# Two regroupings in one kernel: early weights copied behind key tiles, late weights split in place behind attention

## The chip, the cores and the metric

The kernel runs on one core of one Trainium2 chip. The metric is the time of the whole program on the device in microseconds, the median of several runs. TensorE (PE in the rows, its weight load PEld) multiplies, VectorE (DVE), ScalarE (ACT) and GpSimd (POOL) work on elements, and SyncE (SP) issues most of the DMAs.

## The reference: three layers behind each other

```python
# 1. linear attention, 8 batches x 8 heads x 576 tokens x 64
proj = x @ w_phi;  proj -= max(abs(proj))            # x = q, k;  128 features
phi  = concat(exp(proj), exp(-proj))
kv = k_phi^T v;  z = sum(k_phi);  out = (q_phi kv) / (q_phi z + 1e-6)
# 2. four attention experts on d = 512, top 2 of 4 by a gate
logits = x @ w_gate;  w = softmax over the top 2
y_e = softmax(causal(q_e k_e^T / 8)) v_e @ wo_e;     out = sum of w_e * y_e
# 3. token shift, then a gated two-layer map
xk = mu_k*x + (1-mu_k)*x_prev;  xr = mu_r*x + (1-mu_r)*x_prev
r = sigmoid(xr @ w_r);  v = relu(xk @ w_k)**2 @ w_v;  out = r * v
```

All is float32. The kernel keeps accuracy by splitting a float32 operand into a rounded high part (a copy to the type fp32r, mostly on ACT) and a low part (a subtraction on DVE or POOL) and adding three products (`mm3`).

## The kernel before

The program is written as streams of small stages, and `weave` draws from whichever stream is furthest behind. The streams are: `favors` (layer 1, batch by batch, first the keys as `k_unit`, then the queries as `q_unit`), `moe1` (layer 2 up to the values, in tasks `s_task` and `av_task`), `compose` and `decodes` (they build combined weights of layers 2 and 3 and write them to DRAM as `wf` and `wc`), `load_moe1` (the weights of q, k, v of layer 2), `gates_keys` (matmuls `rk`, results in a tile `z`, stored to `kd`), and `moe2` (the last products, `vacc`). A scheduler of the tile framework then puts each engine's instructions into one fixed order. On the chip each engine works through its own order and waits in place for what is not ready; so does the DMA queue on SP.

Three places matter here.

- **The first keys.** A unit covers two tiles of 128 tokens (the third of each five covers one). It loads `raw`, splits it into `hi` (ACT, L97) and `lo` (POOL, L100), projects into `pj` (PE, L288 to L290), takes the absolute maximum `m` and subtracts it to get `pm` (DVE, L298 and L300), takes two exponentials `ph` (ACT, L323 and L324), and multiplies by the values into `kv` (PE, L343). `raw` and `hi` have two buffers each, and the projection has two banks of PSUM, so that unit 3 waits for the subtraction of unit 1. In the same stretch `load_moe1` brings six pieces of weights (`wst1`) and copies each (ACT, 0.6 us) and subtracts (DVE), and `compose` splits `wo` and starts to decode.
- **The late weights.** When layer 1 is done its buffers are closed, the state is called `favored`, and a pool `pW` opens in the same place. Four matrices `wc` (j = 0, 1, 3, 4) are read in eight pieces through two staging buffers (tag `wst2`), copied to `wch` on ACT and subtracted into `wcl` on POOL, by `combo`, all in one go. From then on the third slice of `rk` (`sl == 2`) puts its `z` into the same two staging buffers, while the first and second slices use a ring of four (tag `e`):

```python
if sl == 2 and len(WC) >= 4:
    z = late['pW'].tile([P, 768], F32, name='z', tag='wst2', bufs=2)[:, :HC]
else:
    z = pR.tile([P, HC], F32, name='z', tag='e', bufs=4)
```

- **Attention.** A piece of attention weights `a` is scaled on POOL (L559), transposed on PE (L566), multiplied by the values (`av_task`, L601), and its result is evacuated by ACT into `yc` (in `evac`, L104) and added by DVE (L610).

Of the kernel before, what the change touches and what calls it, by code (L numbers as in the profile page):

```python
# [13 lines left out]
P = 128  # L14
# [62 lines left out]
def fused_kernel(ctx: ExitStack, tc: tile.TileContext, qT, kT, vx, wphi, wq, wk, wvg, wo, mu, w64, ident, cmask, tri, out):  # L77
# [24 lines left out]
    def evac(e, o, i):  # L102
        if e == 'a':
            nc.scalar.activation(o, i, AF.Copy)  # L104
        else:
            nc.vector.tensor_copy(o, i)
    state = {}

    def tg(n):
# [37 lines left out]
    def clear_pads():  # L147
        for t in K2Z:
            nc.gpsimd.memset(t[64:P, 0].bitcast(F32), 0.0)
            nc.gpsimd.memset(t[0:64, 1].bitcast(F32), 0.0)  # L150
        for t in VSP:
            nc.gpsimd.memset(t[64:P, 4].bitcast(F32), 0.0)
        for t in AT1:
            nc.gpsimd.memset(t[64:P, 1280:1600].bitcast(F32), 0.0)
        for t in YF:
            nc.gpsimd.memset(t[:, 0:1], 0.0)

    def load_moe1():
        for src, h, l, n in ((wq, wqh, wql, 'p a b c -> p (a b c)'), (wk, wkh, wkl, 'p a b c -> p (a b c)'), (wvg, wvh, wvl, 'p a b -> p (a b)')):
            hf, lf, sf = (h.rearrange(n), l.rearrange(n), src.rearrange(n))  # L160
            w = hf.shape[1] // 2
            for i in range(2):
                s_ = pA.tile([P, S], F32, name='wst1', tag='a', bufs=3)
                nc.sync.dma_start(s_[:, :w], sf[:, i * w:(i + 1) * w])
                split(hf[:, i * w:(i + 1) * w], lf[:, i * w:(i + 1) * w], s_[:, :w], 'a')
                yield 40

    def decode(pool, i, rawkw, sq, cost=1, pool_raw=None):
# [7 lines left out]
        if sq == 'a':  # L176
            nc.scalar.activation(hz, top, AF.Square)
        else:
            nc.gpsimd.tensor_mul(hz, top, top)
# [28 lines left out]
    def compose():  # L208
        sw = [pR.tile([P, 4, 256], F32R, name='sw', tag=f'y{h}') for h in range(2)]
        for i in range(2):  # L210
            st_ = pR.tile([P, 2, 256], F32, name='wof', tag='e', bufs=4)
            nc.sync.dma_start(st_, wo[:, 2 * i:2 * i + 2])
            split(sw[0][:, 2 * i:2 * i + 2], sw[1][:, 2 * i:2 * i + 2], st_)
            yield 1
# [48 lines left out]
    def favor(b):  # L263
        kvbank = {}

        def proj_stages(src, g, u, dst, first=False):
# [4 lines left out]
            def load():  # L271
                t_ = pF.tile([P, 256], F32, name='raw', tag='raw', bufs=2)
                nc.sync.dma_start(t_[:, :n], src[b, g, :, tl[0] * P:tl[0] * P + n])
                dst['raw'] = t_
# [19 lines left out]
            def norm():  # L294
                g = 2 * nt
                ps = dst['ps'][:, :g * P].rearrange('p (g f) -> p g f', f=P)
                m = pF.tile([P, 4], F32, name='m', tag='m', bufs=3)
                nc.vector.tensor_reduce(m[:, :g], ps, axis=AX.X, op=OP.max, apply_absolute_value=True)  # L298
                pm = pF.tile([P, 512], F32, name='pm', tag='pm', bufs=3)
                nc.vector.tensor_sub(pm[:, :g * P].rearrange('p (g f) -> p g f', f=P), ps, m[:, :g].unsqueeze(2).to_broadcast([P, g, P]))  # L300
                dst['pm'] = pm
# [3 lines left out]
        def k_unit(g, u):  # L305
# [13 lines left out]
            def norm2():  # L319
# [3 lines left out]
                nc.scalar.activation(kp[:, 0, :n], d['pm'][:, :n], AF.Exp)  # L323
                nc.scalar.activation(kp[:, 1, :n], d['pm'][:, :n], AF.Exp, scale=-1.0)  # L324
                d['kp'] = kp

            def kvmm(sel):
# [90 lines left out]
    def moe1():  # L418
# [167 lines left out]
        def av_task(b, e, hf):  # L586
# [19 lines left out]
            def ev():  # L606
                ps = d['ps']
                yc = pA.tile([64, 320], F32, name='yc', tag='a', bufs=3)
                evac('a', yc[:, :W], ps[64:P, :W])
                nc.vector.tensor_add(YF[ep][hr, 1 + q0:1 + q0 + W], ps[0:64, :W], yc[:, :W])  # L610

            def taps():
# [48 lines left out]
    def favors():  # L661
# [14 lines left out]
        state['favored'] = True  # L676
        pW = late['pW'] = ctx.enter_context(tc.tile_pool(name='pW', bufs=1))
        for j in (0, 1, 3, 4):
            for k in range(2):
                combo(j, k, 1, pW, pW, 768, 'wst2', 2)()  # L680
                yield 2000
    WC = {}

    def combo(j, k, n, pool, stage, w, tag, bufs):
# [31 lines left out]
    def gates_keys():  # L716

        def one(c):
# [3 lines left out]
            def unit(n):  # L722
# [9 lines left out]
                def ev():  # L732
                    if sl == 2 and len(WC) >= 4:
                        z = late['pW'].tile([P, 768], F32, name='z', tag='wst2', bufs=2)[:, :HC]
                    else:
# [60 lines left out]
    def moe2():  # L796
# [12 lines left out]
        def first():  # L809
            while not (done.get(0, 0) == NB and B - 1 in read and len(WC) == 4):  # L810
                yield None
# [163 lines left out]
    fs, ms, rk, m2 = (favors(), skewed(moe1()), skewed(gates_keys()), moe2())  # L975
    for _ in range(3):
        next(fs)
    for dst, src in ((idn, ident), (cm, cmask), (trs, tri), (mus, mu)):
        nc.sync.dma_start(dst, src)
    weave(tc, (fs, 0.0, 99.0 * 1000.0, lambda: -1000 if 'favored' in state else 0), (ms, 0.8, 72.0 * 1000.0, lambda: 0), (compose(), 0.35, 206.0 / 2.15, lambda: -1000), (decodes(24, NW), 2.55, 5.0 * 16 / 1.6, lambda: -1000), (load_moe1(), 0.45, 1000.0, lambda: 0), (rk, 2.6, 60.0 * 1000.0, lambda: -1000), (m2, 4.7, 1e6, lambda: 0), until=ms)  # L980
    phA.close()
    state['late'] = True
# [52 lines left out]
```

## Time and profile before

| what | us |
|---|---|
| median of three runs | 1247.85 (1245.38 to 1250.11) |
| the profiled execution | 1247.39 |
| its span on the core | 1245.4 |
| PE busy in the span | 1209.5 (97%) |
| DVE, ACT, POOL busy | 943.0, 817.4, 428.3 |
| chain that ended last | PE 81%, DVE 8%, DMA 4%, ACT 3%, POOL 2% |

The profiled execution lies 0.46 us under the median, and 2.0 us of it lie around the span. PE is busy nearly all the time, so what can be won is found where it sits idle, or where it works at the lower of its two clocks. The page's second part shows both in forty slices.

### The profile page before, as it was taken

The numbers are of one execution on the slowest core, as the hardware profiler recorded it, in microseconds if no ns is written. First come the engines' busy times: TensorE is split into PE (matmuls) and PEld (weight loads), VectorE is DVE, ScalarE is ACT, GpSimd is POOL, SyncE is SP. The second block draws the span as 40 slices with busy tenths as digits, with TensorE's granted clock in tenths as the row PEclk, the third lists the DMA queues.
The fourth block names the chain that finished last, engine by engine and source line by source line (L and its number), as shares of the span: only waits on it lengthen the run. The fifth ranks groups of instructions, "written<-read, shape, count | busy, mean of one in ns | idle before, by whom it ended". The sixth has DMA issues, their size and how long they took to land.

```text
span 1245.4 us, 26673 instructions
## 1 busy us (share of the span) xinstructions
PE 1209.5 (97%) x9014; PEld 1169.1 (94%) x9014; DVE 943.0 (76%) x2493; ACT 817.4 (66%) x2008; POOL 428.3 (34%) x630
## 2 busy tenths in 40 slices
PE   8999999999999999999999999989999999999998
PEld 7899889999999999999999999988898899999998
DVE  7875988878977777886888767857657687756766
ACT  6665767657767776775668767577758585456534
POOL 5541666445643333543444534342211100000000
PEclk9999999989999999999999999999999999999999
DMA  6332134312324444455355443575788998899843
GB/s 206 91 88 86 63 99 154 110 59 83 108 80 147 145 146 122 115 162 157 108 169 177 128 134 119 177 237 156 219 283 279 317 349 301 285 308 304 283 150 127
DMA packets 186919, 212.71 MB, mean 171 GB/s; under 512 B 34464, under 2 KB 170528, under 8 KB 186784
## 3 DMA queue, kind: packets, MB, share of 16 engines
q1 hardware_dynamic: 172960, 192.12, 49.1%
q10 hardware_dynamic: 13824, 18.88, 4.2%
q8 instruction: 73, 1.20, 0.4%
q14 instruction: 62, 0.51, 0.1%
HBM read 145.94 MB, written 65.01 MB: 169 GB/s over the span
## 4 chain that ended last, share of the span: by engine, by line
PE 81%; DVE 8%; DMA 4%; ACT 3%; POOL 2%; issue 2%; SPq 0%; POOLq 0%; ACTq 0%; DVEq 0%
PE rk L117 16%; PE vacc L909 13%; PE kv L343 10%; PE num L386 8%; PE qk L117 6%; PE vp L117 4%; PE yp L601 3%; PE at L566 3%; PE pj L288 3%; PE pj L290 2%; PE pj L289 2%; PE fo L117 2%; PE tq L370 2%; PE sc L528 2%; PE sc L529 2%
## 5 line engine op out<-in xcount | busy, mean ns | idle before, releaser
L559 POOL TENSOR_SCALAR a<-a,sv,gw 128x128 f32<-128x128 f32 (+4 forms) x160 | 107.3, 672 | 228.3 <-DVE sv L553 87.6
L100 POOL TENSOR_TENSOR lo<-raw,hi 128x256 fp32r<-128x256 f32 (+1 forms) x160 | 109.6, 688 | 181.2 <-ACT hi L97 167.9
L386 PE MATMUL num<-kvs,ph 128*128 128x65 f32 (+1 forms) x1280 | 142.0, 262 | 0.6 <-DVE xs L393 0.6
L386 PEld LDWEIGHTS num<-kvs,ph 128*128 128x128 f32 (+1 forms) x1280 | 137.1, 181 | 4.3 <-issue 1.2
L298 DVE TENSOR_REDUCE m<-pj 128x4 f32<-128x512 f32 (+1 forms) x160 | 100.7, 630 | 34.2 <-PE pj L290 32.8
L909 PE MATMUL vacc<-XT,wch 128*128 128x384 f32 x480 | 123.3, 334 | 0.7 <-DVE XT L100 0.7
L741 DVE TENSOR_TENSOR z<-rk,z 128x384 f32<-128x384 f32 x144 | 79.0, 551 | 39.6 <-PE rk L117 27.8
L548 ACT ACTIVATE a<-sc,sv 128x128 f32<-128x128 f32 (+2 forms) x192 | 98.2, 513 | 16.3 <-DVE sv L543 9.2
L300 DVE TENSOR_TENSOR pm<-pj,m 128x512 f32<-128x512 f32 (+1 forms) x160 | 100.1, 629 | 4.5 <-ACT ph L324 1.9
L288 PE MATMUL pj<-wph,hi 128*128 128x256 f32 x288 | 90.0, 313 | 2.7 <-DVE pm L300 1.6
L543 DVE TENSOR_REDUCE sv<-sc 128x1 f32<-128x128 f32 (+2 forms) x192 | 88.4, 468 | 5.0 <-PE sc L529 2.0
L97 ACT ACTIVATE XT<-kx 128x1536 fp32r<-128x1536 f32 x40 | 59.4, 1487 | 47.7 <-PE vacc L909 40.4
L100 DVE TENSOR_TENSOR XT<-kx,XT 128x1536 fp32r<-128x1536 f32 x40 | 70.2, 1754 | 25.7 <-ACT XT L97 25.6
L909 PEld LDWEIGHTS vacc<-XT,wch 128*128 128x128 f32 x480 | 86.8, 188 | 1.1 <-DVE XT L100 1.1
L290 PE MATMUL pj<-wph,lo 128*128 128x256 f32 x288 | 82.3, 286 | 0.3 <-POOL lo L100 0.3
L97 ACT ACTIVATE hi<-raw 128x256 fp32r<-128x256 f32 (+1 forms) x160 | 62.0, 392 | 31.4 <-PE pj L289 9.3
L289 PE MATMUL pj<-wpl,hi 128*128 128x256 f32 x288 | 81.8, 284 | 0.0
L909 PE MATMUL vacc<-XT,wcl 128*128 128x384 f32 x240 | 79.6, 334 | 0.0
L566 PE MATMUL at<-idn,a 128*128 128x128 f32 (+2 forms) x480 | 72.6, 260 | 6.1 <-POOL a L559 5.2
L743 ACT ACTIVATE z<-z 128x384 f32<-128x384 f32 x96 | 50.0, 521 | 34.0 <-DVE z L741 30.5
L582 ACT ACTIVATE at1h<-at 128x384 fp32r<-128x384 f32 (+3 forms) x128 | 53.4, 418 | 25.1 <-PE at L566 17.5
L583 DVE TENSOR_TENSOR at1l<-at,at1h 128x384 fp32r<-128x384 f32 (+3 forms) x128 | 59.1, 462 | 13.9 <-ACT at1h L582 12.4
(531 smaller groups left out, 3696.1 us busy)
## 6 DMA issues: line engine op xcount, KB each, us to landing
wt<-wf SPq DMA_DIRECT2D x216, 256.0 KB, 3.7
kd<-z ACTq DMA_DIRECT2D x96, 192.0 KB, 3.4
kx<-kd SPq DMA_DIRECT2D x21, 768.0 KB, 8.0
yd<-yt SPq DMA_DIRECT2D x16, 864.0 KB, 4.7
kd<-z SPq DMA_DIRECT2D x48, 192.0 KB, 4.4
zs<-kd SPq DMA_DIRECT2D x12, 768.0 KB, 7.5
out_dram<-o SPq DMA_DIRECT2D x24, 384.0 KB, 3.4
raw<-in_kT_dram SPq DMA_DIRECT2D x64, 128.0 KB, 2.3
```

What stands on the lines that cost most here:

```text
L97: nc.scalar.activation(hi, src, AF.Copy)
L100: (el or nc.vector).tensor_sub(lo, src, hi.bitcast(F32))
L117: nc.tensor.matmul(ps, a, m, start=first and i == 0, stop=last and i == n - 1)
L288: nc.tensor.matmul(o, hi[:, c], wph, start=True, stop=False)
L289: nc.tensor.matmul(o, hi[:, c], wpl, start=False, stop=False)
L290: nc.tensor.matmul(o, lo[:, c], wph, start=False, stop=True)
L298: nc.vector.tensor_reduce(m[:, :g], ps, axis=AX.X, op=OP.max, apply_absolute_value=True)
L343: nc.tensor.matmul(bank[:, r, :], d['kp'][:, r % 2, c0:c0 + P], v, start=new and r == 0, stop=end, skip_group_check=True)
L386: nc.tensor.matmul(ps[lo_:hi_, i, j, :], d['qp'][:, hf, c0 + lo_:c0 + hi_], kvs[hp, b][:, r * 65:(r + 1) * 65], start=hf == 0, stop=hf == 1)
L559: eng(asc).tensor_scalar(a[:m, :nk], a[:m, :nk], rc[:m], WT[b][:m, i, e:e + 1], op0=OP.mult, op1=OP.mult)
L566: nc.tensor.transpose(ps[:kw, jj * m:jj * m + m], d['a'][:m, jj * P:jj * P + kw], idn[:m, :m])
L909: nc.tensor.matmul(ps, a[:, f, dp], m[:, f], start=j in (0, 1, 5) and n == 0, stop=n == 11, skip_group_check=True)
```

## The change

Late weights: each of the four `wc` is now loaded whole into its low tile `l` by one DMA of 512 KB, without staging. The eight halves are put on a list. Each `av_task` takes one from the list right after its evacuation `yc`: a copy of `l` into `h` on ACT, ordered behind that evacuation, and a subtraction on POOL that overwrites `l` in place. What is left over at the end of attention is done there. The second and third slices of `rk` get a ring of four `z` of their own in `pW`, and the first slice alone keeps the ring `e`.

Early weights: the first batch's key units leave marks (their subtraction on DVE and second exponential on ACT). The six copies of `load_moe1`, the two splits of `wo` and the first squares of `decode` are ordered behind one mark each, from unit 4 on. The third unit's `raw` is loaded into the tile of `xs`, which is not yet in use, and its load is issued ahead of the constants. Two clears of `vsp` go from POOL to DVE.

```diff
+    marks = []
+    @contextmanager
+    def behind(n):
+        with ExitStack() as es:
+            for ins in marks[n]:
+                es.enter_context(tc.issue_after(getattr(ins, 'ins', ins)))
+            yield
...
         for t in VSP:
-            nc.gpsimd.memset(t[64:P, 4].bitcast(F32), 0.0)
+            nc.vector.memset(t[64:P, 4].bitcast(F32), 0.0)
...
     def load_moe1():
+        k = 4
...
-                split(hf[:, i * w:(i + 1) * w], lf[:, i * w:(i + 1) * w], s_[:, :w], 'a')
+                with behind(k):
+                    split(hf[:, i * w:(i + 1) * w], lf[:, i * w:(i + 1) * w], s_[:, :w], 'a')
+                k += 1
...
-            nc.scalar.activation(hz, top, AF.Square)
+            with behind(6 + i if i < 2 else 9):
+                nc.scalar.activation(hz, top, AF.Square)
...
-            split(sw[0][:, 2 * i:2 * i + 2], sw[1][:, 2 * i:2 * i + 2], st_)
+            with behind(5 + i):
+                split(sw[0][:, 2 * i:2 * i + 2], sw[1][:, 2 * i:2 * i + 2], st_)
...
-                t_ = pF.tile([P, 256], F32, name='raw', tag='raw', bufs=2)
+                extra = first and b == 0 and g == 0 and u == 2
+                t_ = pF.tile([P, 256], F32, name='raw', tag='xs' if extra else 'raw', bufs=1 if extra else 2)
...
+                if b == 0:
+                    marks.append((d['sub'], e_))
...
-                evac('a', yc[:, :W], ps[64:P, :W])
+                last = evac('a', yc[:, :W], ps[64:P, :W])
                 nc.vector.tensor_add(YF[ep][hr, 1 + q0:1 + q0 + W], ps[0:64, :W], yc[:, :W])
+                resplit(getattr(last, 'ins', last))
...
         for j in (0, 1, 3, 4):
+            h, l = (pW.tile([P, 1024], F32R, name=f'wc{x}{j}') for x in 'hl')
+            nc.sync.dma_start(l.bitcast(F32), wc[:, j].rearrange('p q n -> p (q n)'))
+            WC[j] = [x.rearrange('p (f d n) -> p f d n', f=4, d=2) for x in (h, l)]
             for k in range(2):
-                combo(j, k, 1, pW, pW, 768, 'wst2', 2)()
-                yield 2000
+                q = slice(512 * k, 512 * k + 512)
+                late['splits'].append((h[:, q], l[:, q]))
+            yield 2000
+    def resplit(ins=None):
+        if late.get('splits'):
+            h, l = late['splits'].pop(0)
+            with tc.issue_after(ins) if ins is not None else ExitStack():
+                nc.scalar.activation(h, l.bitcast(F32), AF.Copy)
+            nc.gpsimd.tensor_sub(l, l.bitcast(F32), h.bitcast(F32))
...
-                    if sl == 2 and len(WC) >= 4:
-                        z = late['pW'].tile([P, 768], F32, name='z', tag='wst2', bufs=2)[:, :HC]
+                    if sl and 'pW' in late:
+                        z = late['pW'].tile([P, HC], F32, name='z', tag='z', bufs=4)
...
-    for _ in range(3):
+    for _ in range(4):
         next(fs)
...
+    while late['splits']:
+        resplit()
```

The change adds lines, so line numbers of the changed kernel differ: L323 and L324 become L336 and L337, the late copies of L97 become L709, and L743 and L744 become L771 and L772.

ACT, from its first key unit, before (`wqh` and `wkh` are copies of early weights, `hi` and `ph` belong to key units):

```order
L97 ACTIVATE hi<-raw 128x256 x2
L97 ACTIVATE hi<-raw 128x128
L97 ACTIVATE hi<-raw 128x256
L323 ACTIVATE ph<-pm 128x512
L324 ACTIVATE ph<-pm 128x512
L97 ACTIVATE wqh<-wst_879 128x512
L97 ACTIVATE wqh<-wst_975 128x512
L323 ACTIVATE ph<-pm 128x512
L324 ACTIVATE ph<-pm 128x512
L97 ACTIVATE wkh<-wst_1074 128x512
L97 ACTIVATE hi<-raw 128x256
```

The same place now:

```order
L97 ACTIVATE hi<-raw 128x256 x2
L97 ACTIVATE hi<-raw 128x128
L97 ACTIVATE hi<-raw 128x256
L336 ACTIVATE ph<-pm 128x512
L337 ACTIVATE ph<-pm 128x512
L97 ACTIVATE hi<-raw 128x256
L336 ACTIVATE ph<-pm 128x512
L337 ACTIVATE ph<-pm 128x512
L336 ACTIVATE ph<-pm 128x256
L337 ACTIVATE ph<-pm 128x256
L97 ACTIVATE hi<-raw 128x256 x2
L336 ACTIVATE ph<-pm 128x512
```

The copies of `wqh` and `wkh` stood from the first unit's exponentials on; now none of them stands before the fifth unit's.

ACT, where layer 1 has ended, before (`wch` is a copy of a late weight, `a` an exponential of attention, `qs` an evacuation of q):

```order
L97 ACTIVATE wch_13198<-wst_13200 128x512
L97 ACTIVATE wch_13198<-wst_13267 128x512
L548 ACTIVATE a,sv<-sc,sv 64x512
L548 ACTIVATE a,sv<-sc,sv 64x64
L582 ACTIVATE at1h<-at 128x4x128
L451 ACTIVATE qs<-qk 64x288 x4
L582 ACTIVATE at1h<-at 128x4x64
L451 ACTIVATE qs<-qk 64x288 x2
L97 ACTIVATE wch_13330<-wst_13332 128x512
```

The first copy as it stands now, in a later stretch of attention (`yc` is an evacuation of attention, `kd` a store of `z`):

```order
L104 ACTIVATE yc<-yp 64x256
L709 ACTIVATE wch_13198<-wcl_13199 128x512
L773 DMA kd_89<-z 128x384
L597 ACTIVATE at1h<-at 128x4x128
L771 ACTIVATE z<-z 128x384
L563 ACTIVATE a,sv<-sc,sv 128x128
L772 ACTIVATE z<-z 128x384
```

Before, two copies stood behind each other and further ones a few places on; now one stands behind an evacuation, and the next is some twenty rows away.

SP, the loads of late weights, before (`wt` are weights of `rk`, `yc_` its inputs, `wst` the staging buffers):

```order
L689 DMA wst_13411<-wc 128x512
L713 DMA yc__12109<-yd_69 128x2x96 x2
L745 DMA kd_88<-z 128x384
L713 DMA yc__12109<-yd_70 128x2x288 x2
L790 DMA wt<-wf_79 128x2x256
L790 DMA wt<-wf_80 128x2x256
L689 DMA wst_13452<-wc 128x512
L689 DMA wst_13503<-wc 128x512
L790 DMA wt<-wf_81 128x2x256
L689 DMA wst_13568<-wc 128x512
L689 DMA wst_13651<-wc 128x512
```

And now:

```order
L773 DMA kd_88<-z 128x384
L697 DMA wcl_13199<-wc 128x1024
L697 DMA wcl_13265<-wc 128x1024
L697 DMA wcl_13327<-wc 128x1024
L697 DMA wcl_13405<-wc 128x1024
L741 DMA yc__12109<-yd_69 128x2x96 x2
L773 DMA kd_88<-z 128x384
L741 DMA yc__12109<-yd_70 128x2x288 x2
L818 DMA wt<-wf_79 128x2x256
L818 DMA wt<-wf_80 128x2x256
L818 DMA wt<-wf_81 128x2x256
L818 DMA wt<-wf_82 128x2x256
```

Five pieces of 256 KB stood among loads for `rk` (three more a little earlier); now four loads of 512 KB stand in a row, in front of two loads of inputs and of the weights.

The scheduler has worked out all orders anew, so that rows move against each other elsewhere too, above all on PE; the numbers of instructions of each kind on PE are the same.

## Rows read from the trace of the kernel before

**Rows 1.** Windows (length; busy us of PE, PEld, DVE, ACT, POOL; PEclk, DMA, GB/s): the span.

```profile
0.00:26.00 26.00, 21.43 (x134) 19.08 (x135) 18.47 (x35) 15.81 (x36) 14.16 (x27) 0.93 0.73 225
26.00:800.00 774.00, 761.69 (x6294) 737.01 (x6293) 615.81 (x1853) 533.81 (x1445) 367.43 (x546) 1.00 0.40 120
800.00:1000.00 200.00, 186.31 (x1209) 173.63 (x1208) 134.36 (x413) 136.87 (x362) 46.67 (x58) 0.99 0.77 246
1000.00:1245.40 245.40, 240.04 (x1383) 239.38 (x1382) 174.40 (x195) 130.88 (x169) 0.00 (x0) 1.00 0.78 264
```

**Rows 2.** PE in order of time, start: start, length, instruction, idle before and its releaser.

```profile
5.82 0.43 PE L290 MATMUL pj<-wph,lo 128*128 128x256 f32 x1 [0.29 <-POOL lo L100]
8.20 0.36 PE L288 MATMUL pj<-wph,hi 128*128 128x256 f32 x1 [0.96 <-DVE pm L300]
9.66 3.57 PE L343 MATMUL kv<-vx__188,ph 128*128 128x128 f32 x16 [0.66 <-ACT ph L323]
19.02 1.16 PE L343 MATMUL kv<-vx__238,ph 128*128 128x128 f32 x8 [0.56 <-ACT kvs L104]
20.02 1.95 PE L343 MATMUL kv<-vx__268,ph 128*128 128x128 f32 x16
22.52 1.95 PE L343 MATMUL kv<-vx__297,ph 128*128 128x128 f32 x16
```

**Rows 3.** POOL, DVE and ACT in order of time, start.

```profile
3.15 1.04 POOL L152 MEMSET vsp<- 64x512 f32 x2
7.36 0.69 DVE L300 TENSOR_TENSOR pm<-pj,m 128x512 f32<-128x512 f32 x1
7.71 0.31 ACT L97 ACTIVATE hi<-raw 128x128 fp32r<-128x128 f32 x1 [3.03 <-DMA raw<-in_kT_dram]
8.99 0.61 ACT L323 ACTIVATE ph<-pm 128x512 f32<-128x512 f32 x1
10.03 0.61 ACT L97 ACTIVATE wqh<-wst 128x512 fp32r<-128x512 f32 x1
```

**Rows 4.** Windows: the stretch at half clock, and the two fifties after 800 us.

```profile
9.36:12.78 3.42, 3.12 (x14) 3.10 (x15) 2.42 (x5) 3.11 (x7) 0.53 (x1) 0.50 0.83 270
800.00:850.00 50.00, 44.64 (x304) 41.73 (x303) 27.84 (x86) 31.04 (x78) 15.94 (x16) 1.00 0.67 213
850.00:900.00 50.00, 46.60 (x306) 43.39 (x307) 38.04 (x126) 37.59 (x107) 15.21 (x21) 1.00 0.63 193
```

**Rows 5.** ACT in order of time, late: copies of late weights that waited.

```profile
809.48 1.23 ACT L97 ACTIVATE wch<-wst 128x512 fp32r<-128x512 f32 x2 [1.31 <-DMA kd<-z]
817.44 0.63 ACT L97 ACTIVATE wch<-wst 128x512 fp32r<-128x512 f32 x1 [1.55 <-DMA wst<-wc]
823.81 0.63 ACT L97 ACTIVATE wch<-wst 128x512 fp32r<-128x512 f32 x1 [0.74 <-DMA wst<-wc]
```

**Rows 6.** The tile wch: copies on ACT; the tile wcl: subtractions on POOL.

```profile
L97 ACT ACTIVATE wch<-wst x9: 621/631/1072, 809.5 to 1014.4; 128x512 fp32r<-128x512 f32 x8, 128x1024 fp32r<-128x1024 f32 x1
L100 POOL TENSOR_TENSOR wcl<-wst,wch x8: 1277/1292/1421, 810.2 to 832.3; 128x512 fp32r<-128x512 f32 x8
```

**Rows 7.** PE and DVE in order of time, late.

```profile
827.21 1.32 PE L117 MATMUL rk<-yc__12039,wt 128*128 128x384 f32 x6 [0.90 <-ACT z L104]
829.36 0.50 PE L117 MATMUL qk<-XT,wkh 128*128 128x288 f32 x2 [0.82 <-DVE k2z L448]
836.47 0.36 PE L117 MATMUL vp<-wvh,XT 128*128 128x260 f32 x1 [1.72 <-DVE k2z L448]
882.22 1.32 PE L117 MATMUL rk<-yc__11894,wt 128*128 128x384 f32 x6 [1.63 <-DVE z L741]
881.61 0.56 DVE L741 TENSOR_TENSOR z<-rk,z 128x384 f32<-128x384 f32 x1 [1.51 <-DMA kd<-z]
```

**Rows 8.** The page's DMA issues: times, KB each, us to landing.

```profile
wt<-wf SPq DMA_DIRECT2D x216, 256.0 KB, 3.7
```

**Rows 9.** Line 550 on DVE, 800 to 1000 us: durations min, median, max.

```profile
L550 DVE SCALAR_TENSOR_TENSOR sv<-sv x9: 142/152/1048, 811.7 to 989.1; 64x1 f32<-64x1 f32 x9
```

More of the change, by code (lines that the diff above doesn't have):

```diff
@@ L1 @@
-from contextlib import ExitStack
+from contextlib import ExitStack, contextmanager
 import numpy as np
@@ L103, in evac @@
         if e == 'a':
-            nc.scalar.activation(o, i, AF.Copy)
-        else:
-            nc.vector.tensor_copy(o, i)
+            return nc.scalar.activation(o, i, AF.Copy)
+        return nc.vector.tensor_copy(o, i)
     state = {}
+    marks = []
[5 more added lines that the diff above has]
+            yield
     def tg(n):
@@ L299, in norm @@
                 pm = pF.tile([P, 512], F32, name='pm', tag='pm', bufs=3)
-                nc.vector.tensor_sub(pm[:, :g * P].rearrange('p (g f) -> p g f', f=P), ps, m[:, :g].unsqueeze(2).to_broadcast([P, g, P]))
+                dst['sub'] = nc.vector.tensor_sub(pm[:, :g * P].rearrange('p (g f) -> p g f', f=P), ps, m[:, :g].unsqueeze(2).to_broadcast([P, g, P]))
                 dst['pm'] = pm
@@ L323, in norm2 @@
                 nc.scalar.activation(kp[:, 0, :n], d['pm'][:, :n], AF.Exp)
-                nc.scalar.activation(kp[:, 1, :n], d['pm'][:, :n], AF.Exp, scale=-1.0)
+                e_ = nc.scalar.activation(kp[:, 1, :n], d['pm'][:, :n], AF.Exp, scale=-1.0)
                 d['kp'] = kp
+                if b == 0:
+                    marks.append((d['sub'], e_))
             def kvmm(sel):
@@ L677, in favors @@
         pW = late['pW'] = ctx.enter_context(tc.tile_pool(name='pW', bufs=1))
+        late['splits'] = []
         for j in (0, 1, 3, 4):
+            h, l = (pW.tile([P, 1024], F32R, name=f'wc{x}{j}') for x in 'hl')
+            nc.sync.dma_start(l.bitcast(F32), wc[:, j].rearrange('p q n -> p (q n)'))
+            WC[j] = [x.rearrange('p (f d n) -> p f d n', f=4, d=2) for x in (h, l)]
             for k in range(2):
-                combo(j, k, 1, pW, pW, 768, 'wst2', 2)()
-                yield 2000
+                q = slice(512 * k, 512 * k + 512)
+                late['splits'].append((h[:, q], l[:, q]))
+            yield 2000
     WC = {}
+    def resplit(ins=None):
[4 more added lines that the diff above has]
+            nc.gpsimd.tensor_sub(l, l.bitcast(F32), h.bitcast(F32))
     def combo(j, k, n, pool, stage, w, tag, bufs):
@@ L809, in first @@
         def first():
-            while not (done.get(0, 0) == NB and B - 1 in read and len(WC) == 4):
+            while not (done.get(0, 0) == NB and B - 1 in read and ('favored' in state)):
                 yield None
@@ L980, in fused_kernel @@
     weave(tc, (fs, 0.0, 99.0 * 1000.0, lambda: -1000 if 'favored' in state else 0), (ms, 0.8, 72.0 * 1000.0, lambda: 0), (compose(), 0.35, 206.0 / 2.15, lambda: -1000), (decodes(24, NW), 2.55, 5.0 * 16 / 1.6, lambda: -1000), (load_moe1(), 0.45, 1000.0, lambda: 0), (rk, 2.6, 60.0 * 1000.0, lambda: -1000), (m2, 4.7, 1e6, lambda: 0), until=ms)
+    assert 'favored' in state
+    while late['splits']:
+        resplit()
     phA.close()
```

## Prediction

> **What bounds the kernel now.** I read the windows over the whole span first. PE is busy for 1209.5 of 1245.4 us, so the bound is PE, and the question is where it is not working. The first 26 us hold 4.57 us of idle PE, the 774 us after them 12.3 us, the stretch from 800 to 1000 us 13.7 us, and the rest 5.4 us [rows 1]. Per microsecond the ends of layer 1 are the bad places: 18% idle in the first stretch and 7% from 800 to 1000 us, against 1.6% between them. Both parts of the change act in these two places. From 1000 us on PE is so full that an earlier arrival there is carried to the end.
>
> Then I read PE in order of time at the start, and who ended each wait. Before the multiplication of the fourth key unit starts at 20.02 us there are waits of 0.29, 0.96, 0.66 and 0.56 us, 2.47 us in all (one more is under 0.2 us) [rows 2]. The releasers are POOL, DVE and ACT, not PE's own work. A second loss does not show as idle: the granted clock was 0.50 between 9.36 and 12.78 us, the lower of the two levels [rows 4], and the sixteen multiplications that fell into it took 3.57 us, where the same sixteen at 20.02 us took 1.95 us [rows 2]. That is 1.62 us lost. The stretch before it was the one with the waits of 0.96 and 0.66 us.
>
> In the late stretch I read ACT in order of time. It stood three times in front of a copy of a late weight: 1.31 us until a store of `z` had left the staging buffer, 1.55 and 0.74 us until a weight had landed, 3.60 us together [rows 5]. The copies themselves are eight times 0.63 us, 5.0 us [rows 6]. So 8.6 us of ACT's time between 809.5 and 832.2 us went to them, 38% of it, and what stood behind them came late: PE then waited 0.90 us for ACT, and 0.82 and 1.72 us for a DVE instruction that had waited for ACT's copy of `k` [rows 7]. PE idles 5.36 us between 800 and 850 us [rows 4].
>
> **Early part.** Nothing is removed: six copies on ACT of some 0.61 us and their subtractions go from behind the first unit to behind the fifth and later ones, the two splits of `wo` and the first squares likewise. What moves forward is the third unit's `raw`. Its copy on ACT waited 3.03 us and started at 7.71 us, and the exponential of the first unit stands behind it [rows 3]. Two clears, 1.04 us on POOL [rows 3], go to DVE. I cost them at nothing there, and at up to 1.04 us if they hold up the split of `w_phi`, which DVE does next. They let POOL make the first `lo` sooner, for which PE waited 0.29 us [rows 2].
>
> I follow the chain. The subtraction of unit 1 ended at 7.36 + 0.69 = 8.05 us, and its exponential started 0.94 us later, since ACT had two late copies of `raw` in front of it [rows 3]. With `raw` there, I put the subtraction's end at 7.7 to 8.0 us, an exponential of 0.61 us right behind it, and the multiplication at about 8.6 us, where it was 9.66 us. From there on I count PE's work up to the multiplication of the fourth unit in the new order: two whole units at 2.50 us (from 20.02 to 22.52 us, one unit without a wait at full clock [rows 2]), the third unit's two halves at about 1.0 us each (the second shows as 1.16 us with its start), and the projections of two units at 0.8 us each (2.50 less 1.95 us, and some overlap), 8.6 us. So it starts at 17.2 us. Before, it started at 20.02 us with one projection of 0.8 us fewer done, so the gain is 20.8 - 17.2 = 3.6 us. This holds only at full clock. If a stretch at half clock falls there again, 1.62 us of it goes: 2.0 us. Whether it falls is open, since one wait of nearly a microsecond before the third projection stays. I take the middle, 2.8 us, with bounds of 0 (new waits eat it) and 4.1 us (2.47 + 1.62, all that was lost).
>
> What hides the moved copies: a unit takes 2.50 us of PE, and on ACT one `hi` (0.31 us for one tile, say 0.4 us for two) and two exponentials, 0.4 + 2 x 0.61 = 1.6 us, so a copy of 0.61 us fits in each [rows 3]. On SP the loads of `raw` for units four and five now stand ahead of the first values and must wait until `lo` has been made. I expect the values just in time; were they late, the cost is under 1 us, since the first multiplication cannot start before 8.2 us anyway.
>
> **Late part.** The waits within the copies go: the weights lie in `l` before the first copy comes up, and no store of `z` stands in the way. So the stretch at 800 to 850 us gets back its 5.36 us but for the 0.40 us that attention's own chain costs there; I count 4.96 us. The ring of four also removes a wait at 881.6 us: DVE stood 1.51 us until a store of `z` had left one of the two staging buffers, and PE waited 1.63 us for it [rows 7]. Together 6.6 us.
>
> What comes back: eight copies of 0.63 us on ACT and eight subtractions of 1.29 us on POOL [rows 6] now stand in a later stretch of attention, where ACT is busy for 37.6 and DVE for 38.0 of 50 us, and PE loses 3.40 us already [rows 4]. The bounds are 0, if all lies in idle time, and 5.0 us, if each copy delays the next piece of attention. ACT has 12.4 us idle in 50, so most should be covered; I take 2.0 us. The four loads of 512 KB stand in a row on SP ahead of inputs and weights of `rk`; a load of 256 KB there takes 3.7 us to land [rows 8] and five are kept ahead, so I cost it at nothing, and at 3 us if that cover fails. Net gain 4.6 us, bounds -1.4 and 6.6 us.
>
> A row says more of the subtractions. A DVE instruction on a single column, which takes 0.15 us at the median, took 1.05 us at 811.7 us [rows 9], while POOL's first two subtractions into `wcl` ran from 810.2 us on [rows 6]. The Trainium skill ("SBUF — State Buffer", Terms) says that DVE and GpSimd share a pair of ports, that one instruction holds it whole, and that the loser is blocked. The trace agrees in this row. That rule speaks against the change, for it moves the subtractions to where DVE is busier; it is the second rival below.
>
> **Sum.** 2.8 + 4.6 = 7.4 us. The profiled execution took 1247.39 us, 0.46 us under the median of 1247.85 us. Since its stalls are the kernel's own and not the run's, I take the gain from the median: 1240.5 us.
>
> **Rivals.** First, one half is given back. Early, the half clock returns and the copies delay later units; or late, the burst of four loads makes `rk` wait 3 us, or the eight copies cost their full 5.0 us. Either leaves 2 to 4.5 us of gain: 1243.4 to 1246 us, which is no change by what can be told apart. For it speaks that PE already loses 3.40 us where the late copies go [rows 4]; against it, that the two halves are far apart and independent.
>
> Second, slower: the copies and subtractions lengthen attention's chain. Place: the pieces after the eight evacuations. Each piece would pay 0.63 us for the copy in front of its exponential, and 1.29 us in which POOL holds up the scaling of `a` and DVE, 8 x 1.92 = 15.4 us. Against 2.8 + 6.6 = 9.4 us saved this gives 1247.85 + 6.0 = 1253.9 us. It decides from about 1.2 us per piece on (9.4 / 8), if nothing else hides it. For it speaks the 1.05 us row; against it, that before, the same eight subtractions, closer together, show such a delay only once among nine of these instructions [rows 9], and that PE has `rk` to fill with.
>
> Third, the new order eats the gain: the 774 us in the middle hold 12.3 us of idle PE [rows 1], in an order that is worked out anew. If a quarter to a half of that is added, or another stretch at half clock (1.6 us) falls there, 1246 to 1251 us. Nothing in the trace favours a sign; the same could add as much gain, down to 1235 us.
>
> Fourth, the edit doesn't do what it says: `behind` only orders instructions on their own engine, and the loads of the early weights still stand ahead of the fifth unit's `raw`. If these loads were the limit, the early gain would be 0 and the time 1243.3 us; I count it with the first rival, since in 9.36 to 12.78 us the DMA engines have 17% left [rows 4].
>
> **How the numbers follow.** My forecast, with both halves largely there, gets 0.58 and its own range is 1236 to 1243.4 us. The first and fourth rivals get 0.22, the third 0.13 and the second 0.07. A measurement can tell 0.5%, 6.2 us: below 1241.6 us is faster and above 1254.1 us slower. The forecast's range lies to some five sixths below 1241.6 us, weighted towards its middle: 0.49, and the third's good side adds 0.02, so faster 0.51. Slower takes most of the second rival, which lies on the border, and a bad tail of the third: 0.06. The rest, 0.43, is no change. The range of 1235 to 1248.5 us leaves out the second rival, the worse half of the third, and a little at the low end.
>
> **What would show it.** Early: the first exponential before 8.5 us, the multiplication of the fourth unit before 18 us, no wait over 0.5 us on PE between 10 and 26 us, and idle PE of under 3 us in the first 26 us. Late: no wait of ACT's late copies for a DMA, idle PE of 800 to 850 us under 2 us, and no wait of `z` for a store. Idle PE from 800 to 1000 us should fall from 13.7 to about 9 us. I am wrong if the waits on `a` (POOL, L559) grow by more than 5 us between 850 and 920 us, if PE waits for `wt` behind the four loads, or if the middle stretch changes its idle time by more than 4 us.

## The result: 0.8% slower, not 0.6% faster

The changed kernel took 1255.86 us, the median of six runs (1254.24 to 1257.81), beside 1245.24 us for the kernel before on the same chip. The ratio on record is 1.0078, with an interval of 1.0055 to 1.0101; it goes by all the runs, and the two medians alone would give 1.0085. The forecast was 1240.5 us and its range ended at 1248.5 us. It started from the three runs known then, 1247.85 us; from 1245.24 us its gain of 7.4 us would lead to some 1237.8 us. The profiled execution took 1255.81 us, its span is 1254.0 us.

### The profile page after: what moved, and what is told of

It reads as the page before. It is cut to its first block, busy times and chain, and to the rows that moved or that the text cites. A ratio compares the mean times of both kernels' runs of the same rounds, so it can differ in the third digit from the quotient of the medians.

```text
span 1254.0 us, 26706 instructions
## 1 busy us (share of the span) xinstructions
PE 1215.1 (97%) x9014; PEld 1171.6 (93%) x9014; DVE 937.5 (75%) x2495; ACT 814.4 (65%) x2008; POOL 428.9 (34%) x628
## 4 chain that ended last, share of the span: by engine, by line
PE 78%; DVE 9%; ACT 4%; DMA 3%; POOL 2%; issue 2%; SPq 1%; ACTq 0%; POOLq 0%; DVEq 0%
PE rk L124 15%; PE vacc L937 11%; PE kv L358 10%; PE num L401 8%; PE qk L124 7%; PE vp L124 4%; PE yp L616 3%; PE at L581 3%; PE pj L301 3%; PE pj L303 2%; PE pj L302 2%; PE fo L124 2%; PE tq L385 2%; PE sc L543 2%; PE sc L544 2%
## 5 line engine op out<-in xcount | busy, mean ns | idle before, releaser
L97 ACT ACTIVATE hi<-raw 128x256 fp32r<-128x256 f32 (+1 forms) x160 | 62.5, 392 | 39.7 <-PE pj L302 12.7
L97 ACT ACTIVATE XT<-kx 128x1536 fp32r<-128x1536 f32 x40 | 59.2, 1486 | 33.5 <-PE vacc L937 31.4
L771 ACT ACTIVATE z<-z 128x384 f32<-128x384 f32 x96 | 49.7, 522 | 36.3 <-DVE z L769 30.8
L543 PE MATMUL sc<-k,qs 128*128 128x128 f32 (+2 forms) x192 | 64.0, 343 | 4.4 <-ACT a L563 4.2
```

The source lines that it names most:

```text
L97: nc.scalar.activation(hi, src, AF.Copy)
```

## The profile after

The first view gives windows of the changed kernel, with PE alone: the stretch, its length, the busy time (instructions), granted clock, share of DMA time and GB/s. The second gives the same for the kernel before, where [rows 1, 4] don't have it. Both come from one execution of each kernel.

```profile
0.00:26.00 26.00, 20.70 (x135) 1.00 0.61 177
26.00:60.00 34.00, 32.11 (x256) 0.90 0.40 115
26.00:800.00 774.00, 757.38 (x6214) 0.99 0.40 120
670.00:800.00 130.00, 126.85 (x990) 0.97 0.45 130
800.00:850.00 50.00, 47.53 (x337) 1.00 0.67 220
850.00:900.00 50.00, 48.60 (x308) 1.00 0.70 215
900.00:950.00 50.00, 49.12 (x339) 1.00 0.84 259
950.00:1000.00 50.00, 45.03 (x275) 0.97 0.93 303
1000.00:1050.00 50.00, 47.48 (x270) 1.00 0.89 298
```

```profile
26.00:60.00 34.00, 32.10 (x284) 1.00 0.33 94
670.00:800.00 130.00, 130.00 (x1056) 1.00 0.47 140
900.00:950.00 50.00, 47.92 (x309) 0.97 0.90 300
950.00:1000.00 50.00, 47.15 (x295) 1.00 0.89 279
1000.00:1050.00 50.00, 49.27 (x284) 1.00 0.98 340
```

Three places look worse: 26 to 60 us, where the clock is 0.90 and 28 fewer instructions ran; 670 to 800 us, where PE was full before and now idles 3.15 us at a lower clock; and 950 to 1050 us, where it idles 7.49 us after 3.58 us. From 800 to 950 us idle time falls from 10.84 us [rows 4 and the view above] to 4.75 us. Whether the late edits did this, and the loss behind it, is for the experiments.

Idle time alone does not add up to the loss, for a matmul at half clock counts as busy. So I also worked out PE's lag: the time, less the sum over the matmuls started so far of the median spacing (from one start to the next) that matmuls of their form have in the kernel before. It is an estimate; sorting the forms otherwise moves its values by up to 0.7 us. After's lag less before's, in us:

| at us | 26 | 50 | 60 | 600 | 800 | 950 | 1050 |
|---|---|---|---|---|---|---|---|
| after | -0.2 | +4.4 | +2.8 | +0.3 | +9.0 | +1.3 | +9.1 |

The fall between 60 and 600 us is no gain of the change. The profiled execution of the kernel before ran at half clock there, and lost some 3.4 us by it (its view, with PE, PEld, DVE, ACT and POOL):

```profile
272.19:279.02 6.83, 6.83 (x33) 6.83 (x33) 5.52 (x15) 3.49 (x12) 3.79 (x5) 0.50 0.34 104
```

What 800 to 950 us gives back, 950 to 1050 us takes again, so the lag at the end is that of 800 us.

**The start.** ACT and PE of the changed kernel in order of time (start, length, instruction, wait before it and releaser):

```profile
7.88 0.63 ACT L336 ACTIVATE ph<-pm 128x512 f32<-128x512 f32 x1 [0.23 <-DVE pm L313]
8.70 1.55 PE L358 MATMUL kv<-vx__188,ph 128*128 128x128 f32 x10
13.83 0.42 ACT L97 ACTIVATE hi<-raw 128x256 fp32r<-128x256 f32 x1 [2.10 <-DMA raw<-in_kT_dram]
16.49 0.42 ACT L97 ACTIVATE hi<-raw 128x256 fp32r<-128x256 f32 x1 [2.24 <-DMA raw<-in_kT_dram]
19.32 1.95 PE L358 MATMUL kv<-vx__268,ph 128*128 128x128 f32 x16
22.73 0.49 PE L358 MATMUL kv<-vx__297,ph 128*128 128x128 f32 x2 [1.09 <-ACT ph L336]
```

Up to 12 us the start is as forecast: the first exponential at 7.88 us (8.99 before, [rows 3]), the first multiplication at 8.70 us (8.6 forecast), full clock. Then ACT waits twice for `raw`, 2.10 and 2.24 us, and the fourth unit's multiplication, which stands behind their projections on PE, comes at 19.32 us, where 17.2 us was forecast. The fifth unit's then waits 1.09 us for ACT.

**At 40 us.** POOL, PE and DVE of the changed kernel:

```profile
39.94 1.45 POOL L100 TENSOR_TENSOR lo<-raw,hi 128x256 fp32r<-128x256 f32 x2
40.02 0.80 DVE L195 TENSOR_SCALAR da<-hz 128x256 int32<-128x256 int32 x1 [1.60 <-POOL hz L192]
40.85 0.83 DVE L196 SCALAR_TENSOR_TENSOR dc<-hz,da 128x256 int32<-128x256 int32 x1
41.92 0.69 DVE L311 TENSOR_REDUCE m<-pj 128x4 f32<-128x512 f32 x1
42.86 0.69 DVE L313 TENSOR_TENSOR pm<-pj,m 128x512 f32<-128x512 f32 x1
43.69 0.36 PE L301 MATMUL pj<-wph,hi 128*128 128x256 f32 x1 [1.57 <-DVE dn L405]
```

DVE stands 1.60 us at `da`, the decoding of a weight, until POOL has made `hz`. The chain of linear attention (`m`, `pm`) stands behind it, and PE waits 1.57 us. The clock falls right after, and again at 682 and 791 us behind the waits of the next part, as windows of the same kernel show:

```profile
44.00:50.80 6.80, 6.80 (x34) 0.50 0.24 67
682.30:685.70 3.40, 3.40 (x24) 0.50 0.60 138
791.50:794.90 3.40, 3.40 (x17) 0.50 0.16 58
```

Half of the first 6.80 us is lost, 3.4 us. With the wait of 1.57 us that is about what the table adds between 26 and 50 us. By 60 us 2.8 us of it is left, since the kernel before has waits of its own there.

**The middle.** The changed kernel around 678 us in order of time, with one more row of `da` at 788 us, and then the first place before:

```profile
674.35 0.61 POOL L190 TENSOR_TENSOR hz<-w__10982 128x256 f32<-128x256 f32 x1 [3.12 <-DMA w__10982<-in_w_dram]
677.41 0.81 DVE L195 TENSOR_SCALAR da<-hz 128x256 int32<-128x256 int32 x1 [0.32 <-POOL hz L192]
678.26 0.49 DVE L625 TENSOR_TENSOR yf<-yp,yc 64x320 f32<-64x320 f32 x1
678.78 0.46 ACT L97 ACTIVATE yt<-yf 128x288 fp32r<-128x288 f32 x1 [0.80 <-DVE yf L625]
679.15 0.67 ACT L563 ACTIVATE a<-sc,sv 128x512 f32<-128x512 f32 x1
679.96 0.24 PE L543 MATMUL sc<-k,qs 128*64 128x64 f32 x1 [1.10 <-ACT a L563]
787.72 0.29 DVE L195 TENSOR_SCALAR da<-hz 128x256 int32<-128x256 int32 x1 [1.79 <-POOL hz L192]
```

```profile
670.37 0.49 DVE L610 TENSOR_TENSOR yf<-yp,yc 64x320 f32<-64x320 f32 x1 [0.75 <-ACT yc L104]
670.89 0.48 ACT L97 ACTIVATE yt<-yf 128x288 fp32r<-128x288 f32 x1 [0.55 <-DVE yf L610]
671.40 0.69 ACT L548 ACTIVATE a<-sc,sv 128x512 f32<-128x512 f32 x1
673.40 0.60 DVE L184 TENSOR_SCALAR da<-hz 128x256 int32<-128x256 int32 x1
```

It is the same instruction of decoding as at 40 us. Before, `da` came 3 us behind attention's `yf`; now it stands ahead of it and waits for a POOL that itself waited 3.12 us for the weight. ACT's `yt` waits for `yf`, the exponential `a` stands behind `yt`, and PE waits 1.10 us for `a`. At 787.72 us `da` waits again, 1.79 us; PE waits 1.38 us at 788.34 us, and from 791.50 to 794.90 us the clock is at 0.50 a third time. No edit touches this stretch: the new order was worked out from what the marks at the start had shifted.

**Late.** The copies of late weights as a tile (count; min, median, max ns; first and last start), then PE's waits and the chain that ended last (start, length, what):

```profile
L709 ACT ACTIVATE wch<-wcl x8: 617/619/623, 867.0 to 922.4; 128x512 fp32r<-128x512 f32 x8
```

```profile
985.18 0.41 PE L124 MATMUL rk<-yc__14586,wt 128*128 128x384 f32 x1 [2.06 <-DMA yc__14586<-yd]
```

```profile
976.64 3.19 DMA yc__14541<-yd
981.34 4.80 DMA yc__14586<-yd
986.18 3.69 PE rk L124 x11
```

None of the eight copies waits for a DMA any more [rows 5, 6], and 800 to 850 us gives back 2.89 of its 5.36 us. At 976 to 986 us the chain that ended last runs through inputs of the third layer that come back from memory, in a stretch where the DMA engines are 93% busy.

## The experiments

All times are medians. The ratios are those on record, from all runs against the kernel before on the same chip, with their 95% interval; they differ a little from the quotient of two medians.

### Each half alone

The early part alone takes the late edits back, the late part alone the early ones:

```diff
 # early part alone
-            h, l = (pW.tile([P, 1024], F32R, name=f'wc{x}{j}') for x in 'hl')
-            nc.sync.dma_start(l.bitcast(F32), wc[:, j].rearrange('p q n -> p (q n)'))
+                combo(j, k, 1, pW, pW, 768, 'wst2', 2)()
 # late part alone
-                with behind(k):
-                    split(hf[:, i * w:(i + 1) * w], ...
+                split(hf[:, i * w:(i + 1) * w], ...
```

> The early part alone: marks, the third raw, the two clears on DVE; late weights and z as before. Its order is that of the changed kernel up to layer 1's end (about 805 us) on every engine. Theory A (the loss comes from the order that the scheduler works out anew, which the early part alone rewrites): the lag against before at 800 us is 9 us as in the changed kernel, and with before's late stalls the end is near 1254 us. Rival B (the loss is the late part's own): near 1245 us, since the lag at 800 us would be made up. Rival C (the parts hurt each other only together): below 1247 us.

> The late part alone: weights split in place behind attention and the ring of four z. Its order is that of before up to about 805 us on every engine. Theory A: no loss before 805 us, and the gain of some 5 to 8 us between 800 and 950 us is kept at least by half, 1238 to 1242 us. Rival B (the late part gives back at 950 to 1050 us what it wins, through loads of inputs of rk that land late): 1244 to 1247 us. In both PE idle between 800 and 850 us is under 3 us, where it was 5.4 us.

Early alone: 1263.83 us, 1.0136 (1.0108 to 1.0165). Late alone: 1246.12 us, 1.0011 (0.9991 to 1.003). So the early part makes all of the loss, and only in its presence does the late part win anything (1.0136 falls to 1.0078, some 7 us). That late alone idles under 3 us from 800 to 850 us was missed: it idles 4.70 us there, after 5.36 us. Early alone shows the lag of the changed kernel up to 800 us (+9.4) on the same order of instructions, and +15.1 at 1050 us. Late alone has before's order up to some 805 us and gives back what it wins. Two windows of late alone, and then two of early alone:

```profile
800.00:900.00 100.00, 93.05 (x620) 1.00 0.71 225
900.00:1050.00 150.00, 140.09 (x851) 0.98 0.88 290
```

```profile
800.00:950.00 150.00, 143.24 (x954) 0.99 0.73 229
950.00:1050.00 100.00, 90.88 (x534) 0.97 0.94 307
```

Against the kernel before, late alone idles 1.81 us less up to 900 us and 4.25 us more behind; from 800 to 950 us it idles 11.74 us, which is 0.90 us more. Early alone, without any late edit, idles 6.76 us from 800 to 950 us (10.84 us before) and 9.12 us from 950 to 1050 us (3.58 us before). So two thirds of what the changed kernel seems to win from 800 to 950 us, and a loss behind it at least as large as its own, come without the late edits too.

### One early edit alone

```diff
 # n_vsp: two clears go from POOL to DVE, nothing else
-            nc.gpsimd.memset(t[64:P, 4].bitcast(F32), 0.0)
+            nc.vector.memset(t[64:P, 4].bitcast(F32), 0.0)
 # n_marks: the three marks of the change alone
+                with behind(k):              # early weights' copies
+            with behind(5 + i):              # the splits of wo
+            with behind(6 + i if i < 2 else 9):   # decoding's first square
```

> Before with one thing changed that costs nothing by itself: two clears of vsp, 1.04 us in all, on DVE instead of POOL in the first three microseconds. The scheduler rewrites the order of all engines behind it. Theory A: the time moves by some microseconds all the same, anywhere between 1238 and 1256 us, in stretches that have nothing to do with the clears. Rival C' (the order matters little; marks and moved loads make the loss): within 2 us of before.

> Before with the marks alone: copies of early weights, splits of wo and first squares behind key units; raw and clears as before. Theory A: the stretch of 26 to 60 us and those behind it differ from the changed kernel's, with no fixed sign. Rival C (putting decode's square behind a late mark makes DVE wait for it at about 40 us, with PE behind it): the wait of PE on DVE near 42 us and the lower clock after it are there again, a lag of 4 us against before at 60 us.

The clears: 1249.12 us, 1.0026 (1.0006 to 1.0046). The marks: 1257.84 us, 1.0095 (1.0063 to 1.0126). The marks alone make a loss as large as the whole change, and like early alone they idle 8.77 us from 950 to 1050 us. The clears move 1 us of work, and yet they give every engine another order from the first 14 us on; the two together are worth a quarter of a per cent. The interval begins at 0.06%, and the profiled execution, 1246.25 us, does not show where it is lost.

### One thing taken out of the changed kernel

```diff
 # v1_nodec: decoding's mark out
-            with behind(6 + i if i < 2 else 9):
-                nc.scalar.activation(hz, top, AF.Square)
+            nc.scalar.activation(hz, top, AF.Square)
 # v3_nomarks: the other two marks out as well
 # v2b_loads: SP's loads of early weights, wo and decoding's inputs behind the keys' loads (one of three)
+                with tc.issue_after(getattr(raws[min(k + 3, 9)], 'ins', raws[min(k + 3, 9)])):
+                    nc.sync.dma_start(s_[:, :w], sf[:, i * w:(i + 1) * w])
```

> The changed kernel without the mark on decode's squares; copies of early weights and splits of wo stay behind key units. Theory C (the late square makes DVE stand in front of decode at 38 to 40 us, PE waits 1.6 us behind it and the clock falls to its lower level): the lag against before at 60 us falls from +2.8 to below 0. Theory A (order in the long middle): the end may still lie anywhere from 1240 to 1256 us, since all orders behind 10 us are new. Rival (the copies themselves, not decode, load DVE): the wait near 42 us stays.

> The changed kernel with the loads of early weights, of wo and of decode's first inputs put behind the loads of raw of units 6 to 10 on SP. Theory D (the early gain was lost since raw of units 6 and 7 landed late behind 1.5 MB of weights: ACT waited 2.1 and 2.2 us for them, PE 1.1 and 1.1 us): both waits of ACT fall below 0.5 us and the lag at 20 to 26 us is 2 us or more under that of the changed kernel. Rival (the DMA engines or something else hold the units): lag at 26 us within 1 us of the changed kernel's 9.2 us.

> The changed kernel without any mark: the third raw, the clears and the late part stay. Theory C: no wait of DVE on POOL near 40 us and no stretch of the lower clock at 44 to 51 us. Theory A: the order is new again, and 640 to 800 us again costs some microseconds over before (3 to 9), as in the three other new orders. If 640 to 800 us costs under 1 us, that stretch depends on the marks.

Without decoding's mark: 1246.98 us, 1.0018 (1.0002 to 1.0033). Without any: 1247.55 us, 1.002 (1.0004 to 1.0036). With the loads moved: 1251.23 us, 1.0063 (1.004 to 1.0087), with a profiled execution that was some 4 us faster than its median. So the loss needs decoding's mark; without it the gap at 42 us is gone and 670 to 800 us is full (130.00 of 130.00 us). Moving the loads repairs the start, where the lag falls to -3.6 us at 20 us, but the wait at `da` stays (1.56 us) and eats it.

### Decoding's mark alone, and the early part without it

```diff
 # n_dec: the kernel before, with this mark only
+            with behind(6 + i if i < 2 else 9):
+                nc.scalar.activation(hz, top, AF.Square)
 # e7_early_nodec: the early part alone, with this mark out
```

> Before with decode's mark alone: the first squares of decode stand behind the key units 7 to 10, all else as before. Theory C (this mark by itself makes DVE wait in front of decode near 40 us and starts the loss): a wait of DVE on POOL of over 1 us at 36 to 44 us, a wait of PE behind it of over 1 us, and a lag against before of 3 to 5 us at 60 us where a stretch at the lower clock follows, 1.5 us where none does. The end near 1250 us or over. Rival (the copies and decode together overload DVE and ACT there): no such wait, within 2 us of before at 100 us.

> The early part alone without decode's mark. Its order is that of the changed kernel without this mark up to layer 1's end. Theory C: 800 us is reached without the 9 us of the early part, within 2 us of before, and the end is 1243 to 1249 us, 14 us or more under the early part with the mark. Rival (the late part made up for the early one, and would be missed here as it was in the early part alone): 1253 us or over.

The mark alone: 1241.45 us, 0.9982 (0.9962 to 1.0001). The early part without it: 1244.19 us, 0.999 (0.9973 to 1.0007). Each is harmless, and together (the early part alone, 1.0136) they cost 1.4% or some 17 us. That the mark is bad by itself was wrong. DVE of the mark alone shows what differs at 40 us:

```profile
39.75 0.29 DVE L194 TENSOR_SCALAR da<-hz 128x256 int32<-128x256 int32 x1 [1.73 <-POOL hz L191]
40.08 0.43 DVE L195 SCALAR_TENSOR_TENSOR dc<-hz,da 128x256 int32<-128x256 int32 x1
40.50 0.69 DVE L308 TENSOR_REDUCE m<-pj 128x4 f32<-128x512 f32 x1
```

DVE waits as long, but `m` follows 0.75 us behind the start of `da`, where in the changed kernel it took 1.90 us. There a third decoding operation stands in between, and `da` and `dc` took 0.80 and 0.83 us, not 0.29 and 0.43, while POOL ran two `lo`. PE then shows no wait at 42 us, and the clock from 26 to 60 us stays at 1.00.

### The best version, and the ring

Both repairs together (loads behind the keys' loads, decoding's mark out), then that with a ring of two for one slice of `z` in place of the ring of four; the same ring of two in the late part alone:

```diff
 # v5_noz and n_late_noz
-                    if sl and 'pW' in late:
-                        z = late['pW'].tile([P, HC], F32, name='z', tag='z', bufs=4)
+                    if sl == 2 and 'pW' in late:
+                        z = late['pW'].tile([P, HC], F32, name='z', tag='z', bufs=2)
```

> Both corrections in the changed kernel: loads of early weights, wo and decode behind those of raw, and no mark on decode. Theories C and D: lag at 26 us about 6.2 us against 9.4 in before, no wait over 1 us at 38 to 44 us, so the early gain of 3 us is kept to 60 us; the end is 3 us under that of the changed kernel without decode's mark, 1241 to 1244 us, unless the new order takes it. Theory A alone (order decides): no relation, 1240 to 1256 us.

> The same with the ring reduced to two buffers for the third slice. Its order is that of the kernel with the four buffers up to layer 1's end, so up to about 800 us the two agree. Theory E (the ring decides nothing beyond the one wait of 1.6 us): within 2.5 us of it. Rival (the ring of four lets rk run ahead and costs 4 us at 900 to 1050 us): 3 to 5 us faster.

> The late part with the ring reduced: the third slice alone has a z of its own, two buffers as in before, so that only the place of the splits differs from before. Theory E (the late part alone came out even, since it won 2 us at 800 to 900 us, in place of the copies' waits, and lost it in the new order of 900 to 1050 us): 1243 to 1247 us, with PE idle at 800 to 850 us below 4 us. Rival (the ring of four, by letting rk run ahead, made the waits on the weights and inputs of rk at 940 to 1000 us): under 1243 us.

Both repairs: 1241.41 us, 0.9972 (0.9953 to 0.9991). It beats the kernel before by some 3 us, and by its ratio the changed one too. Ring of two: 1242.94 us, 0.9985 (0.9966 to 1.0003). Late part alone with it: 1246.94 us, 1.0031 (1.0009 to 1.0053). By the ratios the ring of four gains some 2 us in both places, but the intervals overlap, so this is not shown. PE of the version with both repairs, at the start:

```profile
16.74 1.95 PE L361 MATMUL kv<-vx__268,ph 128*128 128x128 f32 x16
```

With the loads out of the way, the fourth unit comes at 16.74 us, 3.3 us before the kernel before [rows 2]. The forecast's count of 17.2 us was near for this kernel, not for the one that was changed. By the lag some 1.7 us of it is left at 26 us, after a wait of 2.00 us for ACT at 23.54 us.

### One decoding piece moved back, and the best version without the late part

```diff
 # d_mid: the changed kernel, one piece's step put two places later in the list of work
-        yield cost
+        yield from [cost] * (1 + 2 * (i in (32,)))
```

> The changed kernel with one piece of the decoding put two steps later in the list of work (piece 32 of 40). Up to about 600 us every engine has the order of the changed kernel word for word; from there DVE's first decode operation (da) stands behind yf and dl of the attention's chain, as before the change, and not ahead of them. Theory M (the middle's loss of some 8.7 us is DVE standing at da for GpSimd's hz with yf or m behind it, so that ScalarE's a and then PE's scores wait, and half clock follows): the gaps at 678.86, 680.26 and 788.34 and the half-clock stretches behind them go, PE's busy time in 670 to 800 rises from 126.85 to over 129 of 130, the time falls by 5 to 9 us to 1247 to 1251. The loss at 42 us stays. Rival (the middle is lost to something else that this order shares: the loads of the expert weights or ScalarE's share of work): busy time in 670 to 800 stays under 128, time 1253 to 1258.

> The best version so far (early part without decode's mark, with the loads of the early weights behind the keys' loads; 1241.4 us beside 1244.6) with the late part taken back to the kernel before. Theory (the late part gives back at 940 to 1050 what it wins at 800 to 900, so it is worth nothing): 1240 to 1243 us, same as with it. Rival (the late part is worth its 4.6 us where no other loss covers it): 1245 to 1247 us.

The moved piece: 1247.71 us, 1.0034 (1.002 to 1.0048), where the changed kernel has 1.0078: 0.44% or 5.5 us come back. Its windows, and DVE where `da` now stands behind `yf`:

```profile
26.00:60.00 34.00, 31.43 (x273) 1.00 0.41 122
670.00:800.00 130.00, 128.70 (x1042) 1.00 0.47 140
950.00:1000.00 50.00, 47.13 (x296) 1.00 0.89 279
1000.00:1050.00 50.00, 49.28 (x283) 1.00 0.99 345
```

```profile
676.58 0.49 DVE L625 TENSOR_TENSOR yf<-yp,yc 64x320 f32<-64x320 f32 x1
679.56 0.27 DVE L195 TENSOR_SCALAR da<-hz 128x256 int32<-128x256 int32 x1
```

Between 600 and 800 us the lag grew by some 6 us less, and no half clock fell there; the busy time rose a little less than expected (128.70, not over 129 us). The order of the later pieces moves too, so this is the doing of the place of decoding in the order, not of one instruction alone. From 950 to 1050 us this kernel, with all the late edits, idles 3.59 us, as the kernel before does. So the loss there in the changed kernel goes with the slow middle and not with the late edits; what links the two is not shown. The best version without its late part took 1243.07 us, 0.9989 (0.9976 to 1.0003). Against 0.9972 with it, the late part is worth some 2 us there; the intervals overlap, so neither nothing nor the forecast's 4.6 us is ruled out.

## Why the prediction was wrong

- **The early term (2.8 us).** The step that failed first is that the sum counted PE's work and ACT's copies, and put the arrival of `raw` at nothing. The values came in time, but ACT waited 2.10 and 2.24 us for the `raw` of two later units, whose loads stand on SP behind those of early weights. At 19.32 us the gain was 0.7 us, or 1.5 us with the one projection more that the prediction counts, in place of 3.6 us at full clock; at 26 us it was 0.2 us. The fourth rival named this, and its price (gain 0) was right up to there. With the loads moved and decoding's mark out the step gives 3.3 us, or 4.1 us in the prediction's count, its upper bound.
- **The cover of the moved work.** I counted what the copies cost ACT in each unit and left out what the decoding's mark does on DVE. An instruction that waits on DVE for POOL holds up the `m` and `pm` of linear attention behind it. That made 1.57 us of idle PE at 42 us, and the half clock behind it some 3.4 us more. No step of the sum had the decoding on DVE at all.
- **The middle, taken as zero.** This was the step with the largest error: 8.7 us from 600 to 800 us. The third rival named a new order, at 0.13 and 1246 to 1251 us. The runs show it, with place and instruction: `da` ahead of `yf`; moving one piece of decoding back returns 5.5 us. Its range stopped short of the 1255.86 us, and does not follow from its own terms either: a quarter to a half of 12.3 us, or 1.6 us of half clock, on top of 1240.5 us ends at some 1248 us with both. As a sign of being wrong the prediction gave idle time in the middle that changes by more than 4 us. From 26 to 800 us it grew by 4.3 us, from 12.31 us [rows 1] to 16.62 us, and the half clock came on top, which the sign did not look at.
- **The late term (4.6 us).** The copies' waits for DMAs went as said. The step that failed is that PE's idle time from 800 to 850 us was put down whole to them: late alone gets back 0.66 us there, not 4.96 us, and other waits stand in their place (from 800 to 900 us 1.8 us for POOL's `a` and 1.3 us for DVE's `lg`). The 6.1 us that the changed kernel idles less from 800 to 950 us, and the 3.9 us that it idles more up to 1050 us, are for the most part not the late edits' doing, as early alone and the moved piece show. Alone the late part is worth nothing that can be told from zero; in the best version it may be some 2 us.
- **The second rival**, which ended at 1253.9 us and so nearest to the time, was wrong as a mechanism. The copies run from 867.0 to 922.4 us, and 850 to 950 us idles 2.28 us after 5.48 us. Late alone idles 1.57 us more than before there, not 15.4 us, and PE's waits for the scaling of `a` on POOL fall from 2.3 to 1.3 us.

What stays open: where I looked, the half clock came behind gaps of PE, but not behind each of them. In the kernel with the moved piece, a gap of 0.98 us at 43 us was followed by full clock (1.00 from 26 to 60 us), on the changed kernel's order. So how much of the 10 us between the kernels is waits and how much is clock can differ from one execution to the next. Open is also why decoding's mark and the rest of the early part are harmless apart and cost 1.4% together, beyond what the places shown explain, and what the 0.34% is that the moved piece does not return.

## What to carry to other kernels

Where a list of work is turned into an order for all engines at once, an edit at the start is an edit everywhere: run a nearly neutral move to see what a new order may be worth (here 0.26%) before pricing a gain of that size. Look for an instruction of side work that waits on an engine which the main chain also needs in order; here the length of its wait counted less than what stood between it and the chain's next step. Moving a copy back did not free the start here until its load was moved back on the queue as well. And a stretch that improves in the changed kernel is not yet the edit's doing: here the early part alone had two thirds of what the late stretch seemed to win, without a late edit.

## What was not expected of the hardware

- One PE gap of 1.57 us was followed by 6.8 us at a granted clock of 0.50, which cost twice what the gap did.
- `da` on DVE took 0.80 and 0.81 us beside POOL's work at 40 and 677 us and 0.29 us beside none. The Trainium skill ("SBUF — State Buffer", Terms) says that DVE and GpSimd take a shared pair of ports in turn, each for a whole instruction, and the other is blocked. The trace agrees here, at another instruction than the one the prediction had: the rule named beside the second rival held, in another place.
